# One head's chunk columns from the first to the third visit of each pair of head groups, and two pieces placed later

## The chip, the cores and the metric

The kernel runs on one core of one Trainium2 chip. The metric is the device time of one execution in microseconds; the time before is the median of three runs. A profile of one further execution goes with it. All times below are microseconds (us).

## What is computed

A transformer layer without biases: layer norm, sliding-window attention with 32 heads of 32 columns, a residual, a second layer norm and a dense block with SiLU, and a second residual. There are 2048 tokens of 1024 columns.

```python
H = 32; Dh = D // H; W = 256
scores = jnp.einsum("bhqd,bhkd->bhqk", q, k) * (Dh ** -0.5)
mask = (idx[:, None] - idx[None, :] >= 0) & (idx[:, None] - idx[None, :] < W)
p = _softmax(jnp.where(mask[None, None], scores, -1e9), axis=-1)
o = jnp.einsum("bhqk,bhkd->bhqd", p, v)
h = x + (o.transpose(0, 2, 1, 3).reshape(B, S, D) @ wo)
h2 = h + silu(layernorm(h) @ w1) @ w2
```

Each query sees at most the 256 keys up to its own. The kernel leaves out the subtraction of the row maximum: it takes exponentials of the scaled scores, appends a column of ones to the values, and divides by the sum that this column yields.

## The kernel before, in words

**Blocks and dense groups.** The tokens are cut into four blocks of 512, each of four tiles of 128. TensorE is fed by groups of eight dense matmuls, 128 x 128 against 512 columns, that accumulate into one PSUM bank: values (`v_group`, L255), queries and keys (`qk_group`, L265), the output projection (`wo_group`, L286), and later the dense block. While attention lasts, these groups take turns in three banks, `four[0]` to `four[2]` (`next_acc`, L245); VectorE copies each finished bank away (L257, L267, L289). The fourth, `four[3]`, is called `out` below and takes the output of attention. The last four of the eight banks are `sc`.

**Attention is threaded through the dense groups.** The class `Attention` (L493) holds two tables, `visits` and `pieces`, keyed by a count of dense matmuls. Before each of them `between` (L513) looks the count up and emits what stands there. One count is called a slot here. Instructions run on each engine in the order in which they were written, so this table sets the order on TensorE, ScalarE, VectorE and GpSimd alike.

**Units and heads.** A group is four heads; there are eight groups to a block. From block 1 on (`i >= G`) two groups, `i` and `i + 1`, form a pair, and a pair takes 48 slots from `t = 256 + 48 * p`. There are (NB - 1) * G / 2 = 12 pairs. For each head the scores of one group fall into three sets: X and Y (`unit_xy`, L308), each 512 columns by 128 keys, made of parts of 320, 128 and 64 columns, and C, the chunk columns (`unit_c`, L316): four parts of 128 columns, two for either group of the pair, which need no mask.

**A visit** (`visit`, L337) issues score matmuls (`scores`, L364, L382) and then their exponentials. Four heads of one set (`own`) go to `sc`, one bank for each head; single heads of another set (`more`) go to banks among the other four: `idle`, the bank that the next dense group will write; `behind`, the bank of the group before the running one; and `out`. The visits stand four slots into a dense group, at `t + 4`, `t + 20` and `t + 36`, and each is followed by four more matmuls of its group. A matmul of the scores takes 32 rows and 64 columns of the array, so that four heads and two halves of the keys stand side by side; `scores` sorts them by the column count that already stands ahead for that head, and heads whose bank is in `ahead` (first visit: `idle` and `out`) have the added columns before their own.

In the first visit of a pair, `more` is C of heads 0, 1 and 2; in the second C of head 3 and X of group `i + 1` for heads 0 and 1; in the third X of `i + 1` for heads 2 and 3, in `out` and `behind`, while `idle` is not used. The numbers of score matmuls are 48, 44 and 36.

**Exponentials and masks.** ScalarE takes the heads of `more` in the order of the list (`exp_c`, L323: one activation of 512 columns into `c_ring`; `exp_xy`, L329 and L330: two activations, 384 and 128 columns), and then `own` (L329 and L330, 1536 and 512 columns). GpSimd masks X and Y with `affine_select` (L454), two selects for the heads of `more` if they are X, then four for `own`.

**A piece** (`attn_piece`, L487; `attn_out`, L464) multiplies the exponentials of two heads of one group with the values: 24 matmuls of 33 columns into `out`. Then `attn_norm` (L473) reads `out` on VectorE: a reciprocal (L475) and a multiplication (L476). The second piece of a group also appends a transposing DMA (L484) to the list that `run_late` empties before the next dense group, on SyncE's queue. A pair has four pieces: `(i, 0)`, `(i, 1)`, `(i + 1, 0)`, `(i + 1, 1)`. Piece `(i, 0)` needs heads 0 and 1 of X, Y and C of group `i`.

Of the kernel before, what the change touches and what calls it, by code (L numbers as in the profile page):

```python
# [49 lines left out]
def kernel(  # L50
# [79 lines left out]
    def xbuf(i):  # L130
        return r_e[:, 3072 + 5120 * (i % 2):5632 + 5120 * (i % 2)]

    def ybuf(i):
        return r_e[:, 5632 + 5120 * (i % 2):8192 + 5120 * (i % 2)]
# [160 lines left out]
    def mid_at(i, bank, h):  # L295
        return (h + 2) % 4 if bank == "X" and i % 2 else h
# [11 lines left out]
    def unit_xy(i, odd):  # L308
        q0 = odd * P
        mid, first, last = odd, odd - 2, odd + 2  # L310
        return [
            [(i, mid, q0, q0 + 320, 64), (i, last, q0 + 256, q0 + 384, 384), (i, first, q0, q0 + 64, 0)],
            [(i, mid, q0 + 64, q0 + 384, 128), (i, first, q0, q0 + 128, 0), (i, last, q0 + 320, q0 + 384, 448)],
        ]

    def unit_c(i):  # L316
        pair = (i, i + 1) if (i + 1) % 3 < (i + 2) % 3 else (i + 1, i)
        return [[(ii, kt, q * P, q * P + P, (n * 2 + m) * P)
                 for n, ii in enumerate(pair) for m, (kt, q) in enumerate(((-1, 0), (2, 3)))]] * 2

    def exp_c(i, h, bank):
        lo, hi = sorted(((i + 1) % 3, (i + 2) % 3))
        nc.scalar.activation(out=c_ring[:, lo:hi + 1:hi - lo, h, :], in_=four[bank].rearrange("p (n q) -> p n q", q=256),  # L323
                             func=ACT.Exp, scale=scale)

    def exp_xy(e, banks, h0, h1, m0=0):
        tri, mid = banks[:, :, 0:192], banks[:, :, 192:320]
        tri = bass.AP(tensor=tri.tensor, offset=tri.offset, ap=[*tri.ap[:2], [320, 2], tri.ap[2]])
        nc.scalar.activation(out=tri_of(e)[:, h0:h1, :, 64:256], in_=tri, func=ACT.Exp, scale=scale)  # L329
        nc.scalar.activation(out=full_of(e)[:, m0:m0 + h1 - h0, :], in_=mid, func=ACT.Exp, scale=scale)  # L330

    def select_xy(e, pair):
        four_q = e[:, 1024 * pair:1024 * (pair + 1)].rearrange("p (c q) -> p c q", q=256)
        select(four_q[:, :, 0:P], four_q[:, :, 64:64 + P], False)
        select(four_q[:, :, P:2 * P], four_q[:, :, P:2 * P], True)

    def visit(i, n):  # L337


        now = acc_n[0] % 3  # L340
        idle, behind, out = (now + 1) % 3, (now + 2) % 3, 3
        if n == 0:
            own, e_own = unit_xy(i, 0), xbuf(i)
            more = [(0, idle, unit_c(i)), (1, out, unit_c(i)), (2, behind, unit_c(i))]
        elif n == 1:
            own, e_own = unit_xy(i, 1), ybuf(i)
            more = [(3, idle, unit_c(i)), (0, out, unit_xy(i + 1, 0)), (1, behind, unit_xy(i + 1, 0))]
        else:
            own, e_own = unit_xy(i + 1, 1), ybuf(i + 1)
            more = [(2, out, unit_xy(i + 1, 0)), (3, behind, unit_xy(i + 1, 0))]  # L350
        scores(own, more, {idle, out} if n == 0 else ())
        side = [h for h, _, unit in more if len(unit[0]) == 3]
        for h, bank, unit in more:
            if h in side:
                exp_xy(xbuf(i + 1), four[bank].rearrange("p (h q) -> p h q", h=1), h, h + 1, mid_at(i + 1, "X", h))
            else:
                exp_c(i, h, bank)
        if side:
            select_xy(xbuf(i + 1), side[0] // 2)
        exp_xy(e_own, sc[:], 0, 4)  # L360
        for pair in range(2):
            select_xy(e_own, pair)

    def scores(own, more, ahead):  # L364
        todo = []
        for h in range(4):
            for half in range(2):
                runs = [(sc[:, h, :], own[half])]
                for hh, bank, unit in more:
                    if hh == h:  # L370
                        runs.insert(0 if bank in ahead else 1, (four[bank], unit[half]))
                at = 0
                for bank, parts in runs:
                    for p in parts:
                        todo.append((at, h, half, bank, p))
                        at += p[3] - p[2]
        todo.sort(key=lambda m: m[0])
        for _, h, half, bank, (ii, kt, qa, qb, col) in todo:
            b, g = divmod(ii, G)
            t = b * 4 + kt  # L380
            r0, k0 = h * DH, (t % 4) * P + half * 64
            nc.tensor.matmul(  # L382
                bank[half * 64:half * 64 + 64, col:col + qb - qa],
                lhsT=kT[t // 4][r0:r0 + DH, g, k0:k0 + 64], rhs=qT[b][r0:r0 + DH, g, qa:qb],
                start=True, stop=True, tile_position=(r0, half * 64),
            )
# [28 lines left out]
    def visit_0(k):  # L415

        now = acc_n[0] % 3
        idle, behind, out = (now + 1) % 3, (now + 2) % 3, 3
        m, n = k // 3 * 5, k % 3
        if k == 9:  # L420
            own, more = m, []
        elif n == 0:
            own, more = m, [(0, idle, m + 1), (1, out, m + 1), (2, behind, m + 1)]
        elif n == 1:
            own, more = m + 2, [(3, idle, m + 1), (0, out, m + 3), (1, behind, m + 3)]
        else:
            own, more = m + 4, [(2, out, m + 3), (3, behind, m + 3)]
        scores(unit_0(own), [(h, bank, unit_0(mm)) for h, bank, mm in more], (idle, out))
        for h, bank, mm in more:
            at = POS_0[mm] + 640 * h  # L430
            nc.scalar.activation(out=r_e[:, at:at + 512], in_=four[bank], func=ACT.Exp, scale=scale)
        done = []
        for mm in sorted({mm for _, _, mm in more}):
            heads = [h for h, _, x in more if x == mm]
            if mm % 2:
                select_0(mm, heads[0], heads[-1] + 1)
                if own == mm - 1:
                    done.append((mm, heads[0], heads[-1] + 1))
                else:
                    join_0(mm, heads[0], heads[-1] + 1)  # L440
            elif heads[-1] == 3:
                select_0(mm, 0, 4)
        nc.scalar.activation(out=heads_0(own, 0, 4)[:, :, 0:512], in_=sc[:], func=ACT.Exp, scale=scale)
        step = 2 if own % 2 else 4
        for h in range(0, 4, step):
            select_0(own, h, h + step)
            if own % 2:
                join_0(own, h, h + step)
        for mm, h0, h1 in done:
            join_0(mm, h0, h1)  # L450
# [42 lines left out]
    class Attention:  # L493


        def __init__(self):
            self.seen = 0
            self.visits, self.pieces = {}, {}
            at = [84, 108, *range(132, 260, 16)]
            for k in range(10):  # L500
                self.visits[at[k]] = lambda k=k: visit_0(k)
            gaps = (1, 7), (2, 5), (2, 10), (3, 7), (4, 5), (4, 10), (5, 5), (5, 10), (6, 5), (6, 10), (7, 5), (7, 10), (8, 7), (9, 7)
            for d, (k, late) in enumerate(gaps):
                self.pieces[at[k] + late] = (d // 2, d % 2)
            self.pieces.update({267: (G - 1, 0), 284: (G - 1, 1)})
            for p in range((NB - 1) * G // 2):
                i, t = G + 2 * p, 256 + 48 * p
                for n in range(3):
                    self.visits[t + 4 + 16 * n] = lambda i=i, n=n: visit(i, n)
                for n in range(4):  # L510
                    self.pieces[t + (41, 46, 59, 76)[n]] = (i + n // 2, n % 2)

        def between(self, kt):  # L513
            if self.seen in self.pieces:
# [169 lines left out]
    for g0 in range(0, G, 4):  # L684
        for w in range(2):
            for g in range(g0, g0 + 4):
                run_late()
                n = g0 * 2 + w * 4 + g % 4
# [171 lines left out]
```

## Time and profile before

| | us |
|---|---|
| median of 3 runs | 687.07 |
| lowest and highest | 687.06, 687.23 |
| the profiled execution | 686.78 |
| span of its trace, first to last instruction | 685.1 |

The profile lists for each instruction its start and its length; engines are PE (TensorE's matmuls), PEld (its weight loads), ACT (ScalarE), DVE (VectorE), POOL (GpSimd) and SP (SyncE). A row of the view in order of time gives the start, the length from the first start to the last end of the merged instructions, the engine, the line of the kernel, the operation, the tiles written and read, the shape and the count; in brackets stands how long the engine was idle before, and for whom it waited. A matmul's end is modelled: its row lasts until its result has left the array, and the next may start long before. The pairs run from 89 to 274 us of the span, in which dense groups of values, queries and keys and then of the output projection go by.

### The profile page before, as it was taken

How to read it: one execution, taken by the hardware profiler on the slowest of the kernel's cores; microseconds unless marked ns; L12 is line 12 of the kernel's file. 1: busy time of each engine (PE TensorE's matmuls, PEld its weight loads, DVE VectorE, ACT ScalarE, POOL GpSimd, SP SyncE). 2: the span in 40 equal slices, each digit the busy share in tenths (PEclk: the TensorE clock that was granted, in tenths of full speed). 3: DMA queues.
4: the chain of work that ended last, by engine and by line, in shares of the span. 5: the costliest groups of instructions: out<-in, count | busy, mean ns of one | idle time of the engine just before them, and what ended most of it. 6: DMA issues, size and time to landing. Idle time of an engine off the chain costs nothing.

```text
span 685.1 us, 14587 instructions
## 1 busy us (share of the span) xinstructions
PE 681.3 (99%) x6200; PEld 337.7 (49%) x6200; DVE 295.7 (43%) x617; ACT 235.7 (34%) x397; POOL 161.7 (24%) x287
## 2 busy tenths in 40 slices
PE   9999999999999999999999999999999999999998
PEld 4445555555555555444444444444444444444445
DVE  5287755764444446733416144352233261344111
ACT  7347566767676663023300033200133100233000
POOL 1056866576767665000000000000000000000000
PEclk9999999999999999999999999999999999999999
DMA  8725144124531689864033210023200123100110
GB/s 279 258 47 104 25 63 99 22 49 118 158 94 54 175 269 233 212 245 169 1 118 107 63 36 1 0 94 81 72 1 0 46 79 84 39 1 0 32 38 24
DMA packets 77616, 61.49 MB, mean 90 GB/s; under 512 B 52464, under 2 KB 60656, under 8 KB 77552
## 3 DMA queue, kind: packets, MB, share of 16 engines
q1 hardware_dynamic: 77408, 60.31, 32.3%
q8 instruction: 48, 0.79, 0.5%
q10 hardware_dynamic: 144, 0.26, 0.1%
q14 instruction: 16, 0.13, 0.1%
HBM read 39.85 MB, written 8.39 MB: 70 GB/s over the span
## 4 chain that ended last, share of the span: by engine, by line
PE 99%; DVE 0%; issue 0%
PE bank L265 17%; PE hacc L779 16%; PE hacc L807 15%; PE bank L807 13%; PE bank L779 12%; PE bank L286 8%; PE bank L255 7%; PE bank L464 5%; PE sc L382 2%; PE bank L382 2%; PE bank L596 1%; PE tp L255 1%; PE bank L189 0%; PE tp L548 0%; PE tp L556 0%; DVE r_t L822 0%
## 5 line engine op out<-in xcount | busy, mean ns | idle before, releaser
L454 POOL TENSOR_SCALAR_AFFINE_SELECT r_e<-r_e 128x512 bf16<-128x512 bf16 (+2 forms) x264 | 155.2, 601 | 105.9 <-ACT r_e L329 50.1
L807 PEld LDWEIGHTS <-r_a 128*128 128x128 bf16 x952 | 90.9, 98 | 103.0
L779 PEld LDWEIGHTS <-r_w 128*128 128x128 bf16 x896 | 87.7, 98 | 105.7
L807 PE MATMUL hacc<-r_a 128*128 128x512 bf16 (+2 forms) x532 | 103.7, 357 | 0.0
L807 PE MATMUL bank<-r_a 128*128 128x512 bf16 x420 | 91.8, 379 | 0.0
L779 PE MATMUL hacc<-r_e,r_w 128*128 128x512 bf16 x384 | 84.8, 379 | 0.0
L265 PEld LDWEIGHTS <-r_w 128*128 128x128 bf16 x512 | 45.2, 97 | 47.8
L779 PE MATMUL bank<-r_e,r_w 128*128 128x512 bf16 x288 | 64.4, 379 | 0.0
L265 PE MATMUL bank<-r_t,r_w 128*128 128x512 bf16 x256 | 61.9, 379 | 0.0
L267 DVE CAST r_a<-bank 128x512 bf16<-128x512 f32 x59 | 40.5, 689 | 48.0 <-PE bank L265 39.9
L265 PE MATMUL bank<-r_w 128*128 128x512 bf16 x256 | 59.2, 379 | 0.0
L286 PE MATMUL bank<-r_o,r_a 128*128 128x512 bf16 x256 | 58.9, 379 | 0.0
L329 ACT ACTIVATE r_e<-sc 128x1536 bf16<-128x1536 f32 x36 | 53.3, 1482 | 0.0
L464 PEld LDWEIGHTS <-r_e 128*128 128x128 bf16 x1440 | 45.6, 96 | 15.1
L788 ACT ACTIVATE r_n<-bank 128x512 f32<-128x512 f32 x18 | 10.7, 597 | 117.0 <-PE bank L779 117.0
L464 PE MATMUL bank<-r_a,r_e 128*128 128x33 bf16 x1440 | 46.3, 178 | 0.0
L323 ACT ACTIVATE r_e<-bank 128x512 bf16<-128x512 f32 x48 | 26.1, 597 | 42.8 <-PE bank L382 42.8
L788 ACT ACTIVATE r_n<-hacc 128x512 f32<-128x512 f32 x24 | 14.3, 597 | 75.5 <-PE hacc L779 75.5
L822 DVE SCALAR_TENSOR_TENSOR r_t<-bank,r_t 128x512 bf16<-128x512 f32 x15 | 10.3, 684 | 66.6 <-PE bank L807 66.6
L286 PEld LDWEIGHTS <-r_a 128*128 128x128 bf16 x256 | 23.4, 97 | 25.8
L822 DVE SCALAR_TENSOR_TENSOR r_t<-hacc,r_t 128x512 bf16<-128x512 f32 (+2 forms) x19 | 12.0, 632 | 53.6 <-PE hacc L807 53.6
L382 PEld LDWEIGHTS <-r_a 32*64 32x64 bf16 x1856 | 23.6, 103 | 20.2 <-issue 19.5
(100 smaller groups left out, 594.8 us busy)
## 6 DMA issues: line engine op xcount, KB each, us to landing
r_w<-in_B_w_dram SPq DMA_DIRECT2D x8, 896.0 KB, 5.6
r_a<-in_B_w_dram SPq DMA_DIRECT2D x7, 1024.0 KB, 7.9
r_w<-in_A_wqkv_dram SPq DMA_DIRECT2D x4, 1024.0 KB, 9.3
r_t<-h_dram SPq DMA_DIRECT2D x16, 256.0 KB, 2.9
out_dram<-r_t SPq DMA_DIRECT2D x31, 128.0 KB, 1.7
r_e<-h_dram SPq DMA_DIRECT2D x3, 1024.0 KB, 5.9
r_o<-in_A_x_dram SPq DMA_DIRECT2D x11, 256.0 KB, 4.9
r_a<-in_A_x_dram SPq DMA_DIRECT2D x10, 256.0 KB, 4.2
```

What stands on the lines that cost most here:

```text
L255: nc.tensor.matmul(acc, lhsT=lnT_b[b % 2][:, kt, j * P:(j + 1) * P], rhs=wv[:, kt, c * 512:(c + 1) * 512], start=(kt == 0), stop=(kt == KT ...
L265: nc.tensor.matmul(acc, lhsT=wqk[:, kt, col0:col0 + P], rhs=lnT_b[b % 2][:, kt, :], start=(kt == 0), stop=(kt == KT - 1))
L267: copy(out=(qT, kT)[which][b][:, g, :], in_=acc)
L286: nc.tensor.matmul(acc, lhsT=qT[b][:, g, j * P:(j + 1) * P], rhs=wo[:, g, c * 512:(c + 1) * 512], start=(g == 0), stop=(g == G - 1))
L323: nc.scalar.activation(out=c_ring[:, lo:hi + 1:hi - lo, h, :], in_=four[bank].rearrange("p (n q) -> p n q", q=256), func=ACT.Exp, scale=scale)
L329: nc.scalar.activation(out=tri_of(e)[:, h0:h1, :, 64:256], in_=tri, func=ACT.Exp, scale=scale)
L382: nc.tensor.matmul(bank[half * 64:half * 64 + 64, col:col + qb - qa], lhsT=kT[t // 4][r0:r0 + DH, g, k0:k0 + 64], rhs=qT[b][r0:r0 + DH, g, ...
L454: nc.gpsimd.affine_select(out=dst, in_=src, pattern=[[0, n] for n in dst.shape[1:-1]] + [[sgn, P]], compare_op=ALU.is_ge if upper else ALU ...
L464: nc.tensor.matmul(o_ps[:, qt * 2 + hh, 0:VW], lhsT=chunk_of(i, bank, piece, pair * 2 + hh), rhs=v[:, b * 4 + kt, g * 4 + pair * 2 + hh, : ...
L779: nc.tensor.matmul(acc, lhsT=w1[:, kt, ft * P:(ft + 1) * P], rhs=ln2T[b][:, kt, :], start=(kt == 0), stop=(kt == KT - 1))
L788: nc.scalar.activation(out=th, in_=acc, func=ACT.Tanh, scale=0.5)
L807: nc.tensor.matmul(acc[:, 0:c1 - c0], lhsT=gT[:, ft, j * P:(j + 1) * P], rhs=w2[ft // 4][:, ft % 4, c0:c1], start=(ft == 0), stop=(ft == F ...
```

## The change

It touches three lines. In the first visit of a pair the chunk columns of head 0 are dropped from `more`; head 1 takes `idle` and head 2 `out`, and `behind` is not used. In the third visit the chunk columns of head 0 stand first in `more`, in `idle`. Of the four pieces of a pair, the first moves from `t + 41` to `t + 43` and the second from `t + 46` to `t + 47`, so that they stand 7 and 11 slots behind the third visit instead of 5 and 10.

```diff
         if n == 0:
             own, e_own = unit_xy(i, 0), xbuf(i)
-            more = [(0, idle, unit_c(i)), (1, out, unit_c(i)), (2, behind, unit_c(i))]
+            more = [(1, idle, unit_c(i)), (2, out, unit_c(i))]
         elif n == 1:
             own, e_own = unit_xy(i, 1), ybuf(i)
             more = [(3, idle, unit_c(i)), (0, out, unit_xy(i + 1, 0)), (1, behind, unit_xy(i + 1, 0))]
         else:
             own, e_own = unit_xy(i + 1, 1), ybuf(i + 1)
-            more = [(2, out, unit_xy(i + 1, 0)), (3, behind, unit_xy(i + 1, 0))]
+            more = [(0, idle, unit_c(i)), (2, out, unit_xy(i + 1, 0)), (3, behind, unit_xy(i + 1, 0))]
...
                 for n in range(4):
-                    self.pieces[t + (41, 46, 59, 76)[n]] = (i + n // 2, n % 2)
+                    self.pieces[t + (43, 47, 59, 76)[n]] = (i + n // 2, n % 2)
```

The set `ahead` of the first visit stays `{idle, out}`, which are now heads 1 and 2. The numbers of score matmuls become 40, 44 and 44.

## The prediction

> **What bounds the kernel now.** I read four views in this order: the core's span and clock, the chain that ended last, the waits of TensorE, and then the order of time around one pair of heads groups, engine by engine. The first three answer whether the stretch in which the change lies has anything to win.
>
> ```profile
> core 0: 685.1 us, clock 1.000
> ```
>
> ```profile
> PE 99%; DVE 0%; issue 0%
> ```
>
> ```profile
> PE bank L189 <- DVE eps L169: 1.1, 1, 1.1
> ```
>
> The clock was never lowered. The chain is TensorE from end to end, and the only wait of TensorE in the whole program is 1.1 us at the start. So the time is the sum of what TensorE issues. An edit wins only by shortening that, and it loses whatever wait it puts in front of a TensorE instruction.
>
> The next rows are TensorE alone, from the second visit of the eleventh pair (242.49) to the first visit of the twelfth (252.59). L382 are scores, L464 the pieces, L286 the dense matmuls.
>
> ```profile
> 242.49 0.43 PE L382 MATMUL sc<-r_a 32*64 32x320 bf16 x24
> ...
> 243.08 1.90 PE L286 MATMUL bank<-r_o,r_a 128*128 128x512 bf16 x8
> ...
> 247.25 0.43 PE L382 MATMUL sc<-r_a 32*64 32x320 bf16 x24
> ...
> 247.84 1.25 PE L286 MATMUL bank<-r_o,r_a 128*128 128x512 bf16 x5
> 248.93 0.76 PE L464 MATMUL bank<-r_a,r_e 128*128 128x33 bf16 x24
> 249.53 1.24 PE L286 MATMUL bank<-r_o,r_a 128*128 128x512 bf16 x5
> 250.60 0.76 PE L464 MATMUL bank<-r_a,r_e 128*128 128x33 bf16 x24
> 251.21 1.46 PE L286 MATMUL bank<-r_o,r_a 128*128 128x512 bf16 x6
> 252.59 0.25 PE L382 MATMUL bank<-r_a 32*64 32x128 bf16 x4
> ...
> 253.20 0.39 PE L286 MATMUL bank<-r_o,r_a 128*128 128x512 bf16 x1
> ```
>
> Start to start: the second visit (44 matmuls) takes 0.59, the third (36) 0.59, the first (48) 0.61. A piece takes 0.60 to 0.61. The five dense matmuls between the two pieces take 250.60 - 249.53 = 1.07, so a slot is 0.214 to 0.215. A matmul's row is longer (its end is modelled) than the distance to the next, so a wait below some 0.16 would not show as idle time; I therefore go by distances of starts. These are even, so no wait hides here.
>
> **Part 1: head 0's columns go from the first visit to the third.** Eight score matmuls (two halves by four) and one exponential leave the first visit and come back in the third. No instruction is added or lost: the DVE, GpSimd and DMA instructions stay the same in number. What TensorE pays depends on how a visit's length follows its contents. Eight fewer matmuls (44 to 36) changed nothing visible, 0.59 both; four row groups run side by side, and the length is set by a head that carries own and extra columns, 512 and 512, whether two heads or three do. The nearest row with two such heads is an early visit:
>
> ```profile
> 80.40 0.54 PEld L382 LDWEIGHTS <-r_a 32*64 32x64 bf16 x28 [0.42 <-issue]
> 80.97 1.19 PEld L265 LDWEIGHTS <-r_w 128*128 128x128 bf16 x7
> ```
>
> It took 0.57, with 28 matmuls. So the first visit, with two, will take between 0.57 and 0.61; I take 0.59, a gain of 0.02. The third becomes what the second is now, one head of chunk columns and two of the next group's, 44 matmuls, 0.59: no change, at worst the 0.61 of the first. A pair thus gains 0.02, between a loss of 0.02 and a gain of 0.04. There are (4 - 1) x 8 / 2 = 12 pairs: -0.24 us, from -0.5 to +0.24.
>
> The Trainium skill has another measure of packed matmuls (TensorE: Matmul & The Clock Gate, "Measured speedup vs the span model"): each further tile adds about 4 ns of issue. By it the eight matmuls are worth an estimated 0.03 us on either side, the move is neutral, and the sum below would be 688.4. The trace bears it out only in part, as 36 and 44 matmuls took the same 0.59.
>
> **What the moved exponential waits for, and who waits for it.** ScalarE:
>
> ```profile
> 243.20 0.60 ACT L323 ACTIVATE r_e<-bank 128x512 bf16<-128x512 f32 x1 [1.55 <-PE bank L382]
> ...
> 244.06 0.28 ACT L330 ACTIVATE r_e<-bank 128x128 bf16<-128x128 f32 x1
> ...
> 248.16 0.49 ACT L329 ACTIVATE r_e<-bank 128x384 bf16<-128x384 f32 x1 [1.42 <-PE bank L382]
> ...
> 250.56 0.64 ACT L330 ACTIVATE r_e<-sc 128x512 bf16<-128x512 f32 x1
> ```
>
> In the third visit the idle bank is the next dense group's bank, four slots (0.86) after the visit. Today nothing stands in it; after the change that group's first matmul waits for the exponential of head 0, and behind it on TensorE's queue stands all that follows. The second visit has this very layout: its chunk exponential ran from 0.12 to 0.72 after the dense matmuls resumed (243.08), and the group due at 0.86 was not late. ScalarE had idled 1.42 before the third visit, so it is free. I cost this wait at nothing; its cover is 0.14 less a semaphore.
>
> The other five activations of the third visit slide by one exponential's pitch, about 0.5. The first piece needs the bank `out`; in the second visit that bank's last activation ended 1.26 after the resume, and seven slots are 1.50, so the later slot pays for the slide. (Left at five slots, 1.07, it would wait.) The visit's own scores then leave ScalarE at about 251.7 instead of 251.20, still 0.9 ahead of the next first visit, which rewrites that memory at 252.59.
>
> ```profile
> 250.78 2.63 POOL L454 TENSOR_SCALAR_AFFINE_SELECT r_e<-r_e 128x512 bf16<-128x512 bf16 x4 [0.17 <-ACT r_e L329]
> ```
>
> GpSimd's selects slide by the same 0.5. The first two of these four are done halfway, near 252.1, and after the change near 252.6; the piece that reads them stands seven slots behind the visit of 253.20, near 254.7. Nothing.
>
> **Part 2: the pieces, from 5 and 10 slots behind the third visit to 7 and 11.** The number of dense matmuls is fixed, so shifting costs nothing in itself. But the distance between the two pieces shrinks from five slots to four, and both write the same bank: the second piece's first matmul waits until VectorE has normalized the first. VectorE:
>
> ```profile
> 249.79 0.21 DVE L475 RECIPROCAL recip<-bank 128x8 f32<-128x8 f32 x1
> 250.03 0.42 DVE L476 TENSOR_TENSOR r_n<-bank,recip 128x256 bf16<-128x256 f32 x1
> 251.40 0.21 DVE L475 RECIPROCAL recip<-bank 128x8 f32<-128x8 f32 x1 [0.94 <-PE bank L464]
> 251.64 0.42 DVE L476 TENSOR_TENSOR r_n<-bank,recip 128x256 bf16<-128x256 f32 x1
> 251.98 0.68 DVE L289 TENSOR_TENSOR r_t<-bank,r_a 128x512 bf16<-128x512 f32 x1
> ```
>
> The dense matmuls resume at 249.53; the multiply ends at 250.45, 0.92 later. Five slots are 1.07, so today there are 0.15 to spare. Four slots are 0.86: the multiply is still running when the piece is due. How long after its end TensorE starts, two real waits of the opening show (the second is ScalarE's, for the same kind of signal):
>
> ```profile
> 1.02 0.06 DVE L169 MEMSET eps<- 128x1 f32 x1
> ...
> 1.12 2.93 PE L189 MATMUL bank<-r_e 128*128 128x512 f32 x4 [1.12 <-DVE eps L169]
> ```
>
> ```profile
> 6.35 0.37 ACT L559 COPY r_w<-tp 128x256 bf16<-128x256 bf16 x1 [0.78 <-PE tp L556]
> ...
> 6.77 0.11 PEld L596 LDWEIGHTS <-r_w 128*128 128x128 bf16 x2 [0.41 <-ACT r_w L559]
> ```
>
> 1.12 - 1.08 = 0.04 and 6.77 - 6.72 = 0.05. So the second piece starts 0.92 + 0.05 = 0.97 after the resume instead of at 0.86: a new wait of 0.11 in every pair, 12 x 0.11 = +1.32 us. Its lower end is zero (if the signal came earlier than the row's end). Its upper end adds a weight load, if that too had to wait:
>
> ```profile
> 250.39 0.87 PEld L464 LDWEIGHTS <-r_e 128*128 128x128 bf16 x24
> ```
>
> This load began at 250.39, before the multiply ended at 250.45, so it does not wait for it; were I wrong, 0.1 more a pair, 2.5 us in all. I take 0.11. Queued behind the waiting matmul is all of TensorE, so nothing absorbs it.
>
> Late next: the following first visit writes `out` at once, now five slots behind the second piece instead of six. The multiply of 251.64 ended 0.85 after the resume at 251.21; five slots and the turn into scores are about 1.16. Covered by 0.26. That visit no longer touches the bank of the group before, whose eviction (251.98 to 252.66) therefore ceases to matter. The transposing DMA behind the second piece waits one slot and the new 0.11 more, and SyncE's stores and loads queue behind it; what it writes is read only by the output projection, many groups later. Nothing.
>
> **Sum.** -0.24 + 1.32 = +1.1 us. The profiled execution took 686.78 (span 685.1 and 1.7 around it), so 687.9 in its terms; the median shown is 687.07, 0.3 above it, and the forecast for the median is 687.07 + 1.1 = 688.2. Its own range, with 0.09 to 0.13 for the wait and 0 to 0.03 for the gain, is 687.8 to 688.6. About 0.2% (1.37 us) is what a measurement of this kernel can tell from no change, and the forecast lies just inside that.
>
> **Rivals.**
> *The four slots suffice.* The signal comes before the multiply's reported end, or the normalization starts sooner. It decides at 0.81 after the resume. Then only the gain is left: 687.07 - 0.24 = 686.8. Against it: both rows above show a start after the end, never before.
> *The idle bank is late.* The third visit's first activation today starts 0.32 after the resume (248.16 against 247.84), not 0.12 as in the second. If the moved exponential started there it would end at 0.92 and release the group at 0.97 instead of 0.86: 0.11 a pair, 1.3 more, 689.5, slower by more than 0.2%. It decides when the exponential ends later than 0.81. For it: that row. Against it: a chunk exponential of the same kind starts at 0.12 in the second visit, behind the same order of scores.
> *The empty bank pays.* This would need a TensorE wait on a bank in the first visit that the change ends. That visit exceeds the others by 0.02, which bounds it at 0.24 us for all pairs, already in the sum; for 685.7 or less it would need 0.11 a pair, and no row has it. The Trainium skill (Perfetto Trace Analysis, "Matmul Optimizations") speaks for this rival: it asks that all eight PSUM banks be used to raise parallelism. By that rule the change would gain, and the trace does not agree, as TensorE waits for no bank here.
>
> **How the numbers follow.** Forecast 0.60, four slots suffice 0.17, idle bank late 0.17, the empty bank pays 0.03, some other wait (first piece, ScalarE sliding) of 2 us or more 0.03. Slower by over 0.2% (above 688.44): the late bank, the other wait, and the upper quarter of the forecast, 0.35. Faster by over 0.2%: 0.03. Within: 0.62. The range runs from the first rival's 686.7 to the second's 689.5, which also takes in the upper end of the wait with the gain, 689.3.
>
> **What would show it.** Right: behind the third visit, the run of dense matmuls between the pieces is four and takes 0.97, not 0.86, and the second piece starts 0.05 after the multiply's end; first visit about 0.59; period of a pair longer by 0.09. Wrong: 0.86 there (first rival), or a dense group behind the third visit that starts late and waits for L323 (second rival).

## The result and the profile after

| | before | after |
|---|---|---|
| median of ten runs each on one chip | 687.13 | 688.89 |
| lowest and highest | 686.93, 687.99 | 688.22, 689.61 |
| the profiled execution | 686.78 | 688.53 |
| span of its trace | 685.1 | 686.8 |

The ratio is 1.0025, with a 95% interval from 1.0016 to 1.0033: slower by 1.76 us. That is inside the stated range and slower as forecast, but it is over the 0.2% that the forecast stayed under and beyond the forecast's own range, which ended at 688.6. Two executions of the experiments below, one of 3991.57 us (e2_five_apart) and one of 1416.19 us (e7_columns_only, the profiled one), were disturbed, and neither they nor that profile are used.

The core's line and the head of the chain that ended last show nothing new. TensorE ran at full clock and made up 99% of the chain.

```profile
core 0: 686.8 us, clock 1.000
```

```profile
PE 99%; DMA 0%; DVE 0%; issue 0%; DVEq 0%
```

The list of TensorE's waits also still holds the 1.1 us of the opening alone. The new waits are in the distances of starts. Here is TensorE in order of time from the second visit of the tenth pair to the first visit of the eleventh:

```profile
228.90 0.43 PE L382 MATMUL sc<-r_a 32*64 32x320 bf16 x24
...
229.49 1.90 PE L286 MATMUL bank<-r_o,r_a 128*128 128x512 bf16 x8
...
233.65 0.43 PE L382 MATMUL sc<-r_a 32*64 32x320 bf16 x24
...
234.24 1.76 PE L286 MATMUL bank<-r_o,r_a 128*128 128x512 bf16 x7
235.83 0.76 PE L464 MATMUL bank<-r_a,r_e 128*128 128x33 bf16 x24
236.44 1.02 PE L286 MATMUL bank<-r_o,r_a 128*128 128x512 bf16 x4
237.42 0.75 PE L464 MATMUL bank<-r_a,r_e 128*128 128x33 bf16 x24
238.02 1.24 PE L286 MATMUL bank<-r_o,r_a 128*128 128x512 bf16 x5
239.19 0.32 PE L382 MATMUL sc<-r_a 32*64 32x320 bf16 x2
...
239.76 0.60 PE L286 MATMUL bank<-r_o,r_a 128*128 128x512 bf16 x2
```

The four matmuls between the pieces take 237.42 - 236.44 = 0.98, where four slots are 0.86. The first visit takes 239.76 - 239.19 = 0.57 instead of 0.61. The seven matmuls behind the third visit take 235.83 - 234.24 = 1.59, where the same stretch takes 1.52 in three other pairs: a wait of 0.07 that the sum had at nothing. A view that begins at 235.3 shows the fifth of the seven by itself, the first matmul of the next dense group:

```profile
235.19 0.38 PE L286 MATMUL bank<-r_o,r_a 128*128 128x512 bf16 x1
```

VectorE, the same pair:

```profile
236.70 0.21 DVE L475 RECIPROCAL recip<-bank 128x8 f32<-128x8 f32 x1 [0.64 <-PE bank L464]
236.94 0.42 DVE L476 TENSOR_TENSOR r_n<-bank,recip 128x256 bf16<-128x256 f32 x1
```

The multiplication ends at 237.36 and the second piece starts at 237.42, 0.06 later. ScalarE, the same pair:

```profile
229.60 0.60 ACT L323 ACTIVATE r_e<-bank 128x512 bf16<-128x512 f32 x1 [1.99 <-PE bank L382]
...
234.54 0.60 ACT L323 ACTIVATE r_e<-bank 128x512 bf16<-128x512 f32 x1 [1.40 <-issue]
...
235.40 0.28 ACT L330 ACTIVATE r_e<-bank 128x128 bf16<-128x128 f32 x1
```

The second visit's chunk exponential starts 0.11 after the dense matmuls resumed (229.60 against 229.49). The moved one, in the third visit, starts 0.30 after (234.54 against 234.24) and ends at 235.14. The next dense group, which overwrites the bank that it reads, is due four slots after the resume: in the pairs without a wait its first matmul starts 0.874 after, which is 235.11 here. It started at 235.19, 0.05 behind the exponential's end. The last row ends at 235.68, so the bank `out` is free before the piece at 235.83 and is not what held it.

Twelve pairs added up, from the starts of the two traces:

| stretch | before | after | 12 pairs, us |
|---|---|---|---|
| four slots between the pieces, against 0.861 | five slots, 1.076 | 0.980 | +1.42 |
| first visit | 0.609 | 0.576 | -0.40 |
| third visit | 0.583 | 0.585 | +0.03 |
| second piece | 0.604 | 0.600 | -0.05 |
| seven slots behind the third visit, over 1.521 | none late | 0 to 0.07 late | +0.39 |
| sum | | | +1.39 |

The two profiled executions differ by 688.53 - 686.78 = 1.75, which is 0.36 more. The first visit of the first pair starts at 89.69 after and at 89.36 before: 0.33 of the 0.36 lies ahead of the first changed instruction.

### The profile page after: what moved, and what is told of

It is laid out like the page before. It is cut to its first block, busy times and chain, and to the rows that moved or that the text cites. A ratio compares the mean times of both kernels' runs of the same rounds, so it can differ in the third digit from the quotient of the medians.

```text
span 686.8 us, 14576 instructions
## 1 busy us (share of the span) xinstructions
PE 682.9 (99%) x6200; PEld 337.4 (49%) x6200; DVE 295.3 (43%) x617; ACT 235.7 (34%) x397; POOL 161.2 (23%) x287
## 4 chain that ended last, share of the span: by engine, by line
PE 99%; DMA 0%; DVE 0%; issue 0%; DVEq 0%
PE bank L265 17%; PE hacc L779 16%; PE hacc L807 15%; PE bank L807 13%; PE bank L779 12%; PE bank L286 8%; PE bank L255 7%; PE bank L464 5%; PE sc L382 3%; PE bank L382 1%; PE bank L596 1%; PE tp L255 1%; DMA r_o<-in_A_x_dram 0%; DVE r_e L579 0%; PE tp L548 0%; PE tp L556 0%
```

## The experiments

Theory A: the loss is the wait of the second piece for VectorE, and a smaller one of the idle bank's next group for the moved exponential; the gain is a shorter first visit. Each expectation names the rivals, B or C, that its kernel tells apart. Beside the times stands a second measure: the stretch from the first visit of the first pair to that of the twelfth, eleven pairs in one trace, which the opening does not touch. It was 163.24 before and 164.50 after, and where one kernel was traced twice the two agree within 0.03.

| kernel | time, us | before on that chip | ratio, 95% interval | eleven pairs |
|---|---|---|---|---|
| changed | 688.89 | 687.13 | 1.0025 (1.0016 to 1.0033) | 164.50 |
| e1_pieces_only | 689.51 | 687.43 | 1.0029 (1.0017 to 1.0040) | 165.22 |
| e2_five_apart | 689.11 | 687.43 | 1.0023 (1.0014 to 1.0032) | 164.57 |
| e3_idle_first | 688.32 | 687.43 | 1.0013 (1.0004 to 1.0022) | 164.22 |
| e5_both | 686.98 | 687.43 | 0.9994 (0.9985 to 1.0003) | 162.96 |
| e6_idle_second | 696.92 | 687.49 | 1.0138 (1.0123 to 1.0154) | 171.94 |
| e7_columns_only | 691.28 | 687.49 | 1.0055 (1.0040 to 1.0071) | none |
| e8_four_apart | 688.88 | 687.49 | 1.0019 (1.0011 to 1.0028) | 164.49 |
| e9_idle_first_old | 687.84 | 687.49 | 1.0007 (0.9998 to 1.0016) | 163.84 |
| e10_changed_again | 688.55 | 687.10 | 1.0022 (1.0013 to 1.0031) | 164.53 |
| e11_both_again | 686.75 | 687.10 | 0.9997 (0.9988 to 1.0005) | 162.94 |

**The pieces alone.** The kernel before, with the new places of the pieces and the old visits:

```diff
-                    self.pieces[t + (41, 46, 59, 76)[n]] = (i + n // 2, n % 2)
+                    self.pieces[t + (43, 47, 59, 76)[n]] = (i + n // 2, n % 2)
```

> The kernel before, with the two pieces at 43 and 47 and nothing else. Theory A (two waits of TensorE: the second piece for the normalization, 0.118 a pair, and the dense group behind the third visit for the moved exponential, 0 to 0.075 a pair, against a first visit 0.033 shorter): only the first of these is here, 12 x 0.118 = 1.42, so 688.5 and 0.98 between the pieces. Theory B (the moved columns cost the time, by the longer ScalarE chain, and the pieces' distance is harmless): no change, 687.1. Theory C (the normalization alone, the rest of the difference is chance): 688.5 as well.

It lost 2.08, more than A expected. The wait between the pieces is there, 0.98. A second one stands in the next first visit; TensorE in order of time, then VectorE:

```profile
253.69 1.24 PE L286 MATMUL bank<-r_o,r_a 128*128 128x512 bf16 x5
254.86 0.25 PE L382 MATMUL bank<-r_a 32*64 32x128 bf16 x4
...
255.20 0.24 PE L382 MATMUL bank<-r_a 32*64 32x128 bf16 x2
...
255.54 0.82 PE L286 MATMUL bank<-r_o,r_a 128*128 128x512 bf16 x3
```

```profile
254.46 0.68 DVE L289 TENSOR_TENSOR r_t<-bank,r_a 128x512 bf16<-128x512 f32 x1
```

The visit takes 255.54 - 254.86 = 0.68 instead of 0.61, in all pairs but the first, whose first visit stands ahead of every moved piece. The two waits, 12 x 0.117 and 11 x 0.071, come to 2.2. The eviction of the bank `behind` ends at 255.14, and the scores for that bank start at 255.20, 0.06 later. So the columns' move has a second effect that the prediction named only in passing: with the new pieces, the old first visit would have waited for this eviction.

**The pieces four apart, at 42 and 46,** again with the old visits:

```diff
-                    self.pieces[t + (41, 46, 59, 76)[n]] = (i + n // 2, n % 2)
+                    self.pieces[t + (42, 46, 59, 76)[n]] = (i + n // 2, n % 2)
```

> The kernel before with one number changed: the first piece at 42 instead of 41, so that the two pieces stand four slots apart and the second stays six slots ahead of the first visit. A: only the normalization's wait, 0.12 a pair, first visit 0.61 as before: 687.2 + 1.4 = 688.6, and 0.07 a pair less than with 43 and 47, where the first visit had to wait for the bank of the group before. If that wait of the first visit were also caused by the distance between the pieces, it would show here as well, 0.68, and the time would be 689.5.

```profile
250.73 1.02 PE L286 MATMUL bank<-r_o,r_a 128*128 128x512 bf16 x4
251.71 0.75 PE L464 MATMUL bank<-r_a,r_e 128*128 128x33 bf16 x24
252.31 1.46 PE L286 MATMUL bank<-r_o,r_a 128*128 128x512 bf16 x6
253.70 0.25 PE L382 MATMUL bank<-r_a 32*64 32x128 bf16 x4
...
254.31 0.60 PE L286 MATMUL bank<-r_o,r_a 128*128 128x512 bf16 x2
```

251.71 - 250.73 = 0.98 between the pieces, and a first visit of 254.31 - 253.70 = 0.61. This is the wait between the pieces by itself: +1.39 measured, 0.117 x 12 = 1.40 by the trace. The first visit's wait of e1 is gone with one more slot behind the second piece, so it came from that distance and not from the distance between the pieces.

**The columns alone.** The changed visits, the pieces at their old places:

```diff
-                    self.pieces[t + (43, 47, 59, 76)[n]] = (i + n // 2, n % 2)
+                    self.pieces[t + (41, 46, 59, 76)[n]] = (i + n // 2, n % 2)
```

> The changed visits with the pieces at their old places, 41 and 46. A: the first piece is due 1.09 after the resume but its bank is free only at 1.3 to 1.5 (its two activations stand behind the moved exponential): 0.25 to 0.4 a pair, 3 to 5 us; the normalization's wait is gone (five apart) and the first visit is short: 687.1 - 0.4 + 3 to 5 = 690 to 692. B (columns cost, pieces do not): about 688.9.

It lost 3.79 us. Without a profile of this kernel the reason is inferred from the next kernel's trace: there the first piece cannot start before 1.47 behind the third visit on average, and at five slots it is due at 1.09. That is 0.38 x 12 = 4.5, less the 0.40 of the first visit, so 4.1 by estimate. Neither half of the change is harmless: 2.08 and 3.79 alone, 1.76 together.

**The pieces five apart, at 42 and 47,** with the changed visits:

```diff
-                    self.pieces[t + (43, 47, 59, 76)[n]] = (i + n // 2, n % 2)
+                    self.pieces[t + (42, 47, 59, 76)[n]] = (i + n // 2, n % 2)
```

> The changed kernel with the pieces at 42 and 47, five slots apart again. A: the normalization's wait goes (1.42 less), the exponential's wait stays (about 0.4), and the first piece, six slots (1.29) behind the resume, now waits for the activations of its bank, which end at 1.27 to 1.45: up to 0.2 a pair, some 0.8 in all. 687.1 - 0.4 + 0.4 + 0.8 = 687.9. B: nothing of the pieces matters, 688.9. C: 687.1 - 0.4 = 686.7 plus the same 0.8, 687.5.

```profile
235.13 1.54 PE L286 MATMUL bank<-r_o,r_a 128*128 128x512 bf16 x6
236.63 0.75 PE L464 MATMUL bank<-r_a,r_e 128*128 128x33 bf16 x24
237.23 1.24 PE L286 MATMUL bank<-r_o,r_a 128*128 128x512 bf16 x5
238.31 0.76 PE L464 MATMUL bank<-r_a,r_e 128*128 128x33 bf16 x24
```

```profile
236.29 0.28 ACT L330 ACTIVATE r_e<-bank 128x128 bf16<-128x128 f32 x1
```

The wait between the pieces is gone: five slots take 238.31 - 237.23 = 1.08. But the first piece starts 236.63 - 235.13 = 1.50 behind the third visit instead of 1.30, because the last activation of `out` ends at 236.57. One wait was traded for another of the same size, and the size expected (about 1 us less than the changed kernel) was missed. At 41 and at 42 the first piece waits, and at 43 with 47 the second one does. (43 with 48 was not tried.)

**The idle bank's scores first.** In `scores`, the heads of `ahead` issue their added columns before their own. The third visit had none; here it has its idle bank:

```diff
-        scores(own, more, {idle, out} if n == 0 else ())
+        scores(own, more, {idle, out} if n == 0 else {idle} if n == 2 else ())
```

> The changed kernel with the idle bank's score matmuls issued ahead of their head's own in the third visit, so that its exponential can start some 0.2 earlier. A: the dense group behind the third visit is never late, seven slots always take 1.52, and the wait of 0.118 for the normalization stays: 687.1 - 0.4 + 1.4 = 688.1. B and C: the same as the changed kernel, 688.9.

```profile
233.84 1.68 PE L286 MATMUL bank<-r_o,r_a 128*128 128x512 bf16 x7
235.36 0.76 PE L464 MATMUL bank<-r_a,r_e 128*128 128x33 bf16 x24
235.96 1.02 PE L286 MATMUL bank<-r_o,r_a 128*128 128x512 bf16 x4
236.94 0.75 PE L464 MATMUL bank<-r_a,r_e 128*128 128x33 bf16 x24
```

```profile
233.82 0.60 ACT L323 ACTIVATE r_e<-bank 128x512 bf16<-128x512 f32 x1 [1.09 <-issue]
```

The moved exponential now starts as the dense matmuls resume (233.82 against 233.84) and ends at 234.42, well before the next group is due at 234.71. The seven slots take 1.52 in all twelve pairs. The piece behind still waits, 0.98. Against the changed kernel it gained 0.28 over eleven pairs; the lateness that went was 0.39 over twelve, and eight third visits are 0.01 longer. By time alone the two kernels are not told apart, as their intervals overlap; the trace shows the gain.

**Both waits removed:** the edit of e3 with the pieces of e2.

```diff
-        scores(own, more, {idle, out} if n == 0 else ())
+        scores(own, more, {idle, out} if n == 0 else {idle} if n == 2 else ())
...
-                    self.pieces[t + (43, 47, 59, 76)[n]] = (i + n // 2, n % 2)
+                    self.pieces[t + (42, 47, 59, 76)[n]] = (i + n // 2, n % 2)
```

> The changed kernel with both edits: idle bank first in the third visit, pieces at 42 and 47. A: both waits go, the bank of the first piece is free at about 1.2 and the piece is due at 1.29; only the shorter first visit is left, 687.1 - 0.4 = 686.7, faster than before by 0.06%. B: 688.9, or a little less. C: 686.7 plus up to 0.8 for the first piece.

```profile
248.47 1.47 PE L286 MATMUL bank<-r_o,r_a 128*128 128x512 bf16 x6
249.77 0.76 PE L464 MATMUL bank<-r_a,r_e 128*128 128x33 bf16 x24
250.38 1.24 PE L286 MATMUL bank<-r_o,r_a 128*128 128x512 bf16 x5
251.45 0.76 PE L464 MATMUL bank<-r_a,r_e 128*128 128x33 bf16 x24
```

Six slots take 1.30 and five 1.07: no wait is left, and a pair takes 14.84 instead of 14.87. What remains is the shorter first visit less the longer third. Run again:

> The version without either wait once more, beside the kernel before on the same chip: only the shorter first visit less the third visit's slightly longer scores, 12 x 0.026 = 0.3, so 0.3 to 0.45 faster than before (ratio 0.9993 to 0.9996) and 1.7 faster than the changed kernel.

Both times it was slightly faster than the kernel before, by 0.45 and 0.35, and both times the interval includes 1. By time alone it is not told apart from the kernel before; the traces show eleven pairs shorter by 0.28 and 0.30.

**The exponential of the idle bank second in ScalarE's order,** to give the disputed wait a large dose:

```diff
-            more = [(0, idle, unit_c(i)), (2, out, unit_xy(i + 1, 0)), (3, behind, unit_xy(i + 1, 0))]
+            more = [(2, out, unit_xy(i + 1, 0)), (0, idle, unit_c(i)), (3, behind, unit_xy(i + 1, 0))]
```

> The changed kernel, with head 0's chunk exponential second in the third visit's list, behind the two activations of the bank `out`. This makes the suspected wait of the dense group longer. A (two waits): the exponential runs from about 0.8 to 1.4 after the resume instead of from 0.17-0.30 to 0.76-0.90, so the group due at 0.86 starts at about 1.45; seven slots take about 2.1 instead of 1.52 to 1.59, 0.5 to 0.6 a pair more, 6 to 7 us: 695 to 696. C (the normalization alone, the idle bank never late): 688.9.

```profile
256.05 1.04 PE L286 MATMUL bank<-r_o,r_a 128*128 128x512 bf16 x4
257.65 0.81 PE L286 MATMUL bank<-r_o,r_a 128*128 128x512 bf16 x3 [0.57 <-ACT r_e L323]
```

```profile
257.00 0.60 ACT L323 ACTIVATE r_e<-bank 128x512 bf16<-128x512 f32 x1
```

The exponential ends at 257.60, and the next dense group starts at 257.65 instead of 256.92: 0.72 late, now long enough that the row names its releaser. Over twelve pairs the lateness is 8.5, and with the 1.0 of the other terms (1.39 - 0.39) it gives 9.5. The loss of 9.43 us is larger than expected because the exponential ended 1.44 to 1.57 after the resume, and not at 1.4. So this bank releases the group, 0.05 behind the activation's end, and the lateness goes into the time in full.

**The old places of the pieces, with both early banks first in the third visit:**

```diff
-        scores(own, more, {idle, out} if n == 0 else ())
+        scores(own, more, {idle, out} if n == 0 else {idle, out} if n == 2 else ())
...
-                    self.pieces[t + (43, 47, 59, 76)[n]] = (i + n // 2, n % 2)
+                    self.pieces[t + (41, 46, 59, 76)[n]] = (i + n // 2, n % 2)
```

> The changed visits, with the added columns of idle and out ahead of their heads' own in the third visit too, and the pieces at their old places, 41 and 46. The bank of the first piece is free earlier than in the changed kernel but the piece is due at 1.09. If its last activation ends by 1.04 there is no wait left and the time is 686.7; the changed kernel's end of 1.27 to 1.45, moved forward by the 0.2 of the order, gives 1.07 to 1.25 and a wait of 0 to 0.2 a pair, 687 to 689.

```profile
249.21 1.25 PE L286 MATMUL bank<-r_o,r_a 128*128 128x512 bf16 x5
250.38 0.75 PE L464 MATMUL bank<-r_a,r_e 128*128 128x33 bf16 x24
```

```profile
250.05 0.28 ACT L330 ACTIVATE r_e<-bank 128x128 bf16<-128x128 f32 x1
```

The piece still starts 0.05 behind the last activation of `out` (250.33), at 1.17 instead of 1.09. So even where the first of the three activations starts as the dense matmuls resume, five slots are too few for them, by 0.08. The eleven pairs are 0.60 longer than before; the time, 0.35 longer, has an interval that includes 1.

**The changed kernel once more,** for the part of 1.76 that the pairs do not hold and for the lateness of the exponential:

> The changed kernel once more, beside the kernel before on one chip. The two waits and the shorter first visit add up to 1.4 between the first visit and the last piece in the first profile; the measured difference was 1.8. If the remaining 0.3 to 0.4 belongs to the change, the difference is 1.8 again and the first visit again starts 0.3 later than 89.4; if it is the scatter of the opening loads, the time is nearer to 1.4 (688.6 against 687.2) and the first visit's start differs without any rule. The dense group behind the third visit should be late by other amounts than in the first profile (0 to 0.1 a pair), because its release goes through a separate wait of ScalarE.

It lost 1.45 this time, near the 1.39 of the pairs. The first visit started at 90.06 here, at 89.69 in the first profile, and anywhere from 89.21 to 90.54 among all kernels. The two latest belong to e2, which lost, and to e5, which did not, and all edits lie behind it, so this start follows no edit. The lateness, expected to scatter too, did not: in eleven pairs the moved exponential started within 0.02 of the first profile. The sixth pair's started 0.26 after the resume instead of 0.19. The list of ScalarE's waits, for the changed kernel and then for this run, gives idle time, count and the longest:

```profile
ACT r_e L323 <- PE bank L382: 45.6, 25, 2.6
...
ACT r_e L323 <- issue: 14.9, 11, 1.4
```

```profile
ACT r_e L323 <- issue: 15.0, 11, 1.4
```

Eleven chunk exponentials start behind something other than a TensorE result that the list can name. They are those of the third visit, but for the first pair's. That one waits for TensorE itself; in the changed kernel's first profile it started 0.23 after the resume at 99.46:

```profile
99.69 0.60 ACT L323 ACTIVATE r_e<-bank 128x512 bf16<-128x512 f32 x1 [1.18 <-PE bank L382]
```

## Why the prediction was right and where it failed

**The second piece's wait** was right in mechanism and size: 0.118 a pair against 0.11, 1.42 against 1.32 in all. e8 shows it alone, and e2 shows it gone at five slots. The first rival, that four slots suffice, falls with them.

**The first visit's gain** had the right sign and was mis-sized: 0.033 a pair against 0.02, -0.40 against -0.24. The early visit that the prediction took as its nearest row, 0.57, was the right size, and the middle value of 0.59 was not. The third visit stayed as forecast. The reason given, a head with 512 and 512 columns, covers the third visit alone: one such head more left it as it was, and one fewer shortened the first. Why is open. The 4 ns for each packed matmul of the Trainium skill (TensorE: Matmul & The Clock Gate, "Measured speedup vs the span model") agree in the first visit, where eight fewer saved 0.033, and not in the third, where eight more cost 0.002.

**The step that failed is "I cost this wait at nothing; its cover is 0.14 less a semaphore".** The wait measured 0 to 0.07 a pair, 0.39 in all. The step took the start of the second visit's exponential, 0.12 behind the resume, for the third visit's, which was 0.17 to 0.30. The second rival took the 0.32 at which the third visit's first activation started before. Its condition, an end later than 0.81, was met in nine pairs (0.83 to 0.90). In eight of them the group was late by 0.03 to 0.07, in the ninth by less than 0.01, so its price of 0.11 was too high. That row was in part luck: over the twelve pairs that start lay between 0.16 and 0.33 before, and it does not say which pairs are late after; only the means, 0.27 and 0.25, are alike. e3 shows that this wait goes with an earlier start, and e6 that it grows with a later one.

Why the start is late the trace shows in part, as it also records when TensorE's signals (its semaphore updates) arrive. In the second visit the exponential waits for TensorE itself and starts 0.12 after the resume; the signal is recorded at 0.14. In the third visit of eleven pairs a separate semaphore instruction ahead of the activation waits for VectorE and TensorE, and the activation waits for ScalarE's own earlier work. There it starts 0.03 behind the recorded signal instead of 0.02 ahead of it: 0.05 later. The rest is the signal, which comes at 0.14 to 0.27, though the last score matmul ends by 0.07 in both visits. In the first pair's third visit there is no separate wait, and the start is late all the same, 0.23, with the signal at 0.25; in the second pair's there is one with the signal at 0.14, and the start is 0.17 and the group not late. So the separate wait alone makes no group late; without its 0.05 the latest group, in the tenth pair, would by estimate still be late by 0.02 instead of 0.07. Why TensorE's signal comes later in most third visits stays open, and no kernel changed that alone.

**What was costed at nothing and held:** the first piece at seven slots (nothing but the idle bank delays it), and the next first visit, whose bank `out` was free. The loss of e7 bears out that the first piece would wait if left at five slots. "That visit no longer touches the bank of the group before, whose eviction (251.98 to 252.66) therefore ceases to matter" proved more than a remark: e1 puts it at 0.07 a pair.

**The sum.** The pairs without the late bank were longer by 14.95 - 14.865 = 0.085, and 0.09 was forecast; the others by 0.12 to 0.16. The terms come to 1.39. In the profiled executions the rest is the start of the first pair, which scattered by up to 1.3 us between kernels without following any edit; for the medians that is not shown, but the second measurement was 1.45. So the 0.62 given to "within 0.2%" hung on a term of 0.39: without it, by the trace, the change costs about 1.0, and e3, which is without it, measured 0.89. That the forecast of 1.1 lies so near to this 1.0 is in part luck: the second piece's wait came out 0.10 larger and the first visit's gain 0.16 larger, and the two offset each other.

**The empty bank** paid only through the shorter first visit. The rule that all eight PSUM banks be used (the Trainium skill, Perfetto Trace Analysis, "Matmul Optimizations") gave no gain here that the times can tell: the changed kernel, which uses the empty one, is slower, and with both waits mended (e5, e11) it is not told apart from the kernel before.

## What to carry to other kernels

Where one engine is the bound and its matmul rows overlap, read waits from the distances of starts: none of the waits that made up this loss stands in the list of waits. When work moves to another place in the program, look at the rows that stand at that place now, in several repetitions, and not only at a like instruction elsewhere: here they lay between 0.16 and 0.33, against 0.12. And two edits that each cost alone may pay for each other in part, so test each with the other held: here the order of issue inside the visit and one slot for one piece turned 1.76 lost into nothing that the times can tell.

## What the runs showed of the hardware

Where ScalarE's activation waited for TensorE itself, it started 0.02 ahead of the time at which the trace records TensorE's signal (0.12 against 0.14, and 0.23 against 0.25). Where a semaphore instruction of its own held that wait, it started 0.03 behind (0.17 against 0.14, and 0.30 against 0.27). The signal itself was recorded 0.07 behind the end of the last score matmul in the second visits of the changed kernel, and 0.07 to 0.20 behind it in the third. In the rows shown, TensorE started 0.05 to 0.06 behind the end of the row that released it, VectorE's and ScalarE's alike.
